# Decode attention on one core: where the K and V loads of the third, and the V load of the last step are split, and how many unused matmuls two early steps run

## The chip, the core and the metric

The kernel runs on one core of one Trainium2 chip. Its time is the device time of one execution in microseconds (us). A core has a matmul engine (TensorE, PE in the profile), three engines for other arithmetic (VectorE or DVE, ScalarE or ACT, GpSimd or POOL), a fifth that only issues transfers here (SyncE or SP), and 16 DMA engines that carry what is issued. SBUF is the core's working memory, PSUM the small memory that TensorE writes to.

## The reference

One decoding step of two layers side by side, for a batch of two and a single new token each:

```python
xn = layernorm(x)                                   # x: 2 x 1 x 512
q  = (xn @ wq) as [2, 32, 1, 128]
p  = softmax(q . k_cache * 128**-0.5)               # k_cache: 2 x 32 x 8192 x 128, bf16
o  = p @ v_cache                                    # v_cache: the same shape
out = x + o.reshape(2, 1, 4096) @ wo + relu(xn @ w1) @ w2
```

The two caches hold 134 MB each. The weights have 4.2 MB (wq), 4.2 MB (wo), and 1.8 MB each for w1 and w2.

## The kernel before, in words

The 64 pairs of batch and head are taken four at a time (U = 4), in NP = 16 steps. The code counts them t = 0 to 15, so the "third step" is t = 2. In a step, each of the 128 partitions holds 256 key rows (KB = 256) of one pair: a K tile `ks` and a V tile `vs`, 8.39 MB each. There is one buffer for each, called its slot. There is no second one, so a K tile can be loaded only once the step before has finished with its own.

What TensorE does in a step (lines 306 to 351, one hardware loop, rolled up):

- It waits for the K tile: `dK[0]` before the first half of the transposes, `dK[1]` before the second half.
- 256 transposes (L275) turn the K rows so that the head dimension lies on partitions. They come in 32 groups of 8; VectorE and ScalarE copy each group from PSUM to SBUF (L429). The last transpose of each group counts up a semaphore; group 7, 15, 23 and 31 of a step count up `pT[7]`, so it grows by four in each step.
- 256 score matmuls (L282), with a maximum over each half of the scores (VectorE, L476), then exponentials on ScalarE (L550).
- 256 output matmuls (L335) with V rows as weights. They wait for `dV[0]` before the first half, `dV[1]` before the second. The last matmul of each half counts up `sW`.
- Unless it is the last or last but one step, 24 matmuls of 128x512 into a PSUM tile that nobody reads (L346): the "unused matmuls". `reg` counts the steps from 1, so in step t it holds t + 1.

SyncE issues all loads, one after the other, in an unrolled list (L184 to L194), all into one DMA queue: K of step t, then V of step t. Each issue first waits until the slot is free. `load` (L176) makes either one transfer of the whole tile, once `pT[7]` (for K) or `sW` (for V) says that the whole slot is used up, or two transfers of half a tile, each once its half is used up. `KSPLIT` and `VSPLIT` name the steps whose tiles come in halves. Where a tile comes whole, GpSimd passes its arrival on to the second semaphore (L239), so that TensorE's loop body can be the same in all steps.

Before the loop, wq is loaded into the V slot and q is computed, so V of step 0 waits for that. After the last step's transposes, w1, w2 and wo are loaded into the K slot (wo in four pieces, the later ones smaller), and the end of the program computes both output products and the sum.

## Time and profile before

| | |
|---|---|
| median of 4 runs | 659.97 us (658.18 to 660.2) |
| the profiled execution's own time | 659.18 us |
| its span, first to last instruction | 657.4 us |
| DMA queue 1, share of 16 engines' span | 99.0% |
| read from HBM | 280.50 MB, 427 GB/s over the span |
| TensorE busy, share of the span | 602.5 us, 92% |
| transposes L275, busy | 234.6 us, 4096 |
| output matmuls L335, busy | 141.9 us, 4096 |
| score matmuls L282, busy | 132.5 us, 4096 |
| unused matmuls L346, busy | 74.8 us, 336 |
| mean granted TensorE clock | 0.964 |

A busy time of TensorE is a sum of modelled, pipelined spans; it doesn't mean that the array works at its peak. The DMA rows give the share of time in which the 16 DMA engines have a packet under way. An idle engine matters only if it is on the chain that ends last, so the profile's chain of waits, its stretches of time and its list of what SyncE issued are what the steps below are read from. Times inside the run are counted from the start of the span. The profiled execution's time lies 1.8 us above its span.

### The profile page before, as it was taken

To read this page: it belongs to the slowest core of one execution; us is meant where nothing else is said; L and a number is where in the kernel's file an instruction comes from. 1 tells how busy PE (TensorE), PEld (TensorE's weight loads), DVE (VectorE), ACT (ScalarE), POOL (GpSimd) and SP (SyncE) were. 2 spreads that over 40 slices of the span, in tenths; PEclk is the share of its full clock that TensorE was granted. 3 is DMA by queue.
4 is the path that set the end of the run, shared out by engine and by line. 5 is a ranking of instruction groups with operands and counts; after the bars stand their busy time and mean duration, and the time that the engine had idled before them with its cause. 6 is when DMAs were issued, how large, how long until landed. Compare 5 with 4: busy or idle time off the path is not lost.

```text
span 657.4 us, 27600 instructions
## 1 busy us (share of the span) xinstructions
PE 602.5 (92%) x12987; PEld 547.4 (83%) x12987; DVE 261.9 (40%) x503; ACT 290.9 (44%) x532; POOL 7.2 (1%) x30
## 2 busy tenths in 40 slices
PE   2797999999999999999999999999999999999997
PEld 0596887978889898888979878897987889798987
DVE  1441450716235071632507154260715417072721
ACT  1332443636345263543527354343725435372730
POOL 2000000000000000000000000000000000000000
PEclk9977999999899899999989999998999999999997
DMA  9999999999999999999999999999999999999996
GB/s 381 446 441 425 408 423 447 419 443 439 415 443 431 439 443 419 431 439 439 439 411 435 447 439 435 411 439 447 439 431 411 443 447 439 427 411 435 423 428 281
DMA packets 6223, 280.66 MB, mean 427 GB/s; under 512 B 706, under 2 KB 708, under 8 KB 964
## 3 DMA queue, kind: packets, MB, share of 16 engines
q1 hardware_dynamic: 6208, 280.50, 99.0%
q8 instruction: 8, 0.13, 0.1%
q14 instruction: 3, 0.02, 0.0%
q10 hardware_dynamic: 4, 0.00, 0.0%
HBM read 280.50 MB, written 0.00 MB: 427 GB/s over the span
## 4 chain that ended last, share of the span: by engine, by line
PE 65%; DMA 31%; DVE 2%; issue 1%; SPq 0%; ACT 0%; ACTq 0%
PE tp L275 34%; DMA ks<-in_A_k_cache_dram 27%; PE ot L335 13%; PE Sc L282 11%; PE ms L346 6%; DMA ks<-in_A_wo_dram 4%; DVE mcol L476 2%; PE ms L294 0%; PE ms L300 0%; ACT L429 0%; ACT kT L429 0%; PE Sc L400 0%; SPq L194 0%; SPq L191 0%; SPq L182 0%
## 5 line engine op out<-in xcount | busy, mean ns | idle before, releaser
L429 DVE COPY kT<-tp 128x1024 bf16<-128x1024 bf16 x320 | 209.3, 688 | 252.1 <-PE tp L275 246.5
L275 PEld LDWEIGHTS tp<-identb,ks 128*128 128x128 bf16 x4096 | 232.2, 99 | 16.8 <-DMA ks<-in_A_k_cache_dram 14.9
L275 PE MATMUL tp<-identb,ks 128*128 128x128 bf16 x4096 | 234.6, 220 | 11.4 <-DMA ks<-in_A_k_cache_dram 10.4
L429 ACT COPY kT<-tp 128x1024 bf16<-128x1024 bf16 x192 | 188.2, 1014 | 122.6 <-PE tp L275 122.6
L335 PE MATMUL ot<-prm,vs 128*128 128x64 bf16 x4096 | 141.9, 198 | 2.1 <-issue 2.1
L335 PEld LDWEIGHTS ot<-prm,vs 128*128 128x128 bf16 x4096 | 137.7, 101 | 4.1 <-issue 2.3
L282 PE MATMUL Sc<-q,kT 128*128 128x64 bf16 (+8 forms) x4096 | 132.5, 191 | 1.6 <-issue 1.6
L282 PEld LDWEIGHTS Sc<-q,kT 128*128 128x128 bf16 x4096 | 128.0, 97 | 3.0 <-issue 1.7
L346 PE MATMUL ms<-identb 128*128 128x512 bf16 x336 | 74.8, 379 | 0.0
L476 DVE TENSOR_REDUCE mcol<-Sc 32x1 bf16<-32x128 f32 x128 | 37.1, 289 | 90.2 <-PE Sc L282 88.9
L550 ACT ACTIVATE prm<-Sc,nm 32x128 bf16<-32x128 f32 x128 | 69.0, 539 | 5.4
L545 ACT COPY nm<-ms 128x4 f32<-128x4 f32 x32 | 5.2, 163 | 137.9 <-PE ms L300 137.9
L346 PEld LDWEIGHTS ms<-identb 128*128 128x128 bf16 x336 | 31.9, 98 | 36.4
L561 ACT COPY OTf<-ot 128x8 f32 x16 | 2.7, 166 | 80.2 <-PE ot L335 80.2
L550 ACT ACTIVATION_READ_ACCUMULATOR prm<-Sc,nm x128 | 32.1, 250 | 0.0
L294 PE MATMUL ms<-identb,mcol 128*1 128x128 bf16 x32 | 6.9, 217 | 22.1 <-DVE mcol L476 22.1
L294 PEld LDWEIGHTS ms<-identb,mcol 128*1 128x1 bf16 x32 | 2.5, 79 | 23.9 <-issue 23.1
L429 ACT ACT_TABLE_LOAD x16 | 20.5, 1283 | 3.6 <-issue 3.5
L254 PE MATMUL ot<-vs,xz 128*16 128x512 bf16 x32 | 8.5, 431 | 8.6 <-DMA vs<-in_A_wq_dram 8.6
L483 DVE TENSOR_REDUCE mx<-ms 1x4 bf16<-1x128 bf16 x32 | 8.9, 279 | 13.8 <-PE ms L294 13.8
L254 PEld LDWEIGHTS ot<-vs,xz 128*16 128x16 bf16 x32 | 3.1, 99 | 13.6 <-issue 10.7
L236 POOL COPY q<-qb 128x4 bf16<-128x4 bf16 x16 | 3.0, 188 | 591.4 <-PE Sc L282 573.2
(61 smaller groups left out, 47.5 us busy)
## 6 DMA issues: line engine op xcount, KB each, us to landing
ks<-in_A_k_cache_dram SPq DMA_DIRECT2D x4, 4096.0 KB, 22.9
vs<-in_A_v_cache_dram SPq DMA_DIRECT2D x4, 4096.0 KB, 21.8
vs<-in_A_wq_dram SPq DMA_DIRECT2D x1, 4096.0 KB, 12.2
ks<-in_B_w_dram SPq DMA_DIRECT2D x2, 1792.0 KB, 16.5
ks<-in_A_wo_dram SPq DMA_DIRECT2D x1, 2304.0 KB
ks<-in_A_wo_dram SPq DMA_DIRECT2D x1, 1024.0 KB, 25.9
ks<-in_A_wo_dram SPq DMA_DIRECT2D x1, 512.0 KB, 26.6
ks<-in_A_wo_dram SPq DMA_DIRECT2D x1, 256.0 KB, 26.8
```

The lines of the kernel that those rows point to most:

```text
L236: g.tensor_copy(q4[:], qb[:, U * t:U * t + U]).then_inc(sQ1, 1)
L254: i = pe.matmul(qp, lhsT=xz[:, kt, Z - g * Bsz:Z - g * Bsz + QG * Bsz], rhs=vs[:, (kt * QG + g) * 512:(kt * QG + g + 1) * 512], start=(g = ...
L275: t = pe.transpose(tp[e % 4][:, i, :], ks[:, kk * Dh:(kk + 1) * Dh], identb[:])
L282: t = pe.matmul(Sc[:, U * kk:U * (kk + n)], lhsT=kT[e][:, i, :], rhs=rep(q4[:], n), start=True, stop=True,)
L294: pe.transpose(trp[:, i * P:(i + 1) * P], mcol[:, i:i + 1], identb[:]).then_inc(sT, 1)
L335: t = pe.matmul(oh[:, i, :], lhsT=vs[:, kk * Dh:(kk + 1) * Dh], rhs=rep(prm[:, kk, :], REP), start=(first == 0), stop=(first == KB // 2 - 1),)
L346: pe.matmul(ms[:], lhsT=identb[:], rhs=identb[:].rearrange("p (o k) -> p o k", o=1).to_broadcast([P, 4, P]), start=True, stop=True,)
L429: fn(kT[e][:], tp[e % 4][:]).then_inc(kR[e % HG], 1)
L476: m = v.tensor_reduce(out=mcol[own, i:i + 1], in_=S[own, i * KB // 2:(i + 1) * KB // 2, u], axis=AX.X, op=ALU.max,)
L483: v.tensor_reduce(out=mx[:, i, :], in_=trp[:, i * P:(i + 1) * P].rearrange("o (u m) -> o u m", u=U), axis=AX.X, op=ALU.max, negate=True,). ...
L545: a.copy(nm[:, i, :], bc[:, i, :]).then_inc(sN, 1)
L550: x = a.activation(out=prm[own, k, u], in_=S[own, k, u], func=ACTF.Exp, bias=nm[own, i, u:u + 1], scale=1.0, accum_out=RS[own, i, bass.ds( ...
```

## The change

K2 and V2 (step t = 2) come in two halves, each asked for when that half of its slot is used up. V15 comes whole. TensorE runs 18 unused matmuls in step 0, none in step 1, and 24 in steps 2 to 13 as before. The loop body gets two more branches; the matmuls move into a helper.

```diff
-    KSPLIT = (0, NP - 1)
-    VSPLIT = (1, NP - 1)
+    KSPLIT = (0, 2, NP - 1)
+    VSPLIT = (1, 2)
...
+        def warm(n):
+            for i in range(n):
+                pe.matmul(
+                    ms[:], lhsT=identb[:],
+                    rhs=identb[:].rearrange("p (o k) -> p o k", o=1).to_broadcast([P, 4, P]),
+                    start=True, stop=True,
+                )
...
             with pe.If_lt(reg, NP - 1):
-                for i in range(WARM):
-                    pe.matmul(
-                        ms[:], lhsT=identb[:],
-                        rhs=identb[:].rearrange("p (o k) -> p o k", o=1).to_broadcast([P, 4, P]),
-                        start=True, stop=True,
-                    )
+                with pe.If_ne(reg, 2):
+                    warm(WARM - WARM // 4)
+                    with pe.If_ne(reg, 1):
+                        warm(WARM // 4)
             advance(pe, regs)
```

## The prediction

> Steps are numbered t = 0 to 15 as in the code's loops; K1 is the K tile of step 1, K2a the first half of K2. Added or lost time is in us.

> **What bounds the kernel.** First I read the DMA rows of the page.

> ```profile
> DMA  9999999999999999999999999999999999999996
> ...
> q1 hardware_dynamic: 6208, 280.50, 99.0%
> ...
> HBM read 280.50 MB, written 0.00 MB: 427 GB/s over the span
> ```

> One queue carries everything and its packets fill 99.0% of the span, so only time in which that queue runs dry can be won or lost. Next, stretches of the span (columns: busy us of each engine with its count, granted clock, DMA share, GB/s).

> ```profile
> 90.00:95.00 5.00, 5.00 (x157) 4.81 (x154) 1.44 (x5) 0.16 (x1) 0.00 (x0) 1.00 0.98 406
> 95.00:127.00 32.00, 29.42 (x597) 26.11 (x594) 13.89 (x25) 17.89 (x32) 0.19 (x1) 1.00 1.01 436
> ...
> 170.00:605.00 435.00, 414.28 (x8994) 377.03 (x8991) 177.72 (x338) 203.38 (x382) 2.26 (x12) 0.97 1.00 433
> ```

> From 170 to 605 us the queue runs at 433 GB/s without a hole; a K or V tile is 8.39 MB, so it takes 19.36 and a step of two tiles 38.7. Around 90 to 95 us, 406 GB/s shows a hole. The chain of waits and SyncE's issues say why:

> ```profile
> 73.74 14.31 PE tp L275 x256
> 88.06 24.17 DMA ks<-in_A_k_cache_dram
> ...
> 126.78 24.16 DMA ks<-in_A_k_cache_dram
> 150.94 0.05 issue
> 150.98 14.47 PE tp L275 x256
> ```
> ```profile
> 88.06 0.33 SPq L182 DMA_DIRECT2D ks<-in_A_k_cache_dram  x1
> 105.94 0.33 SPq L182 DMA_DIRECT2D vs<-in_A_v_cache_dram  x1
> 126.78 0.33 SPq L182 DMA_DIRECT2D ks<-in_A_k_cache_dram  x1
> 144.65 0.33 SPq L182 DMA_DIRECT2D vs<-in_A_v_cache_dram  x1
> 165.48 0.33 SPq L182 DMA_DIRECT2D ks<-in_A_k_cache_dram  x1
> ```

> The K slot is single: K2 is asked for when step 1's transposes end (88.06), K3 at 126.78, K4 at 165.48. The trace's packet records, followed on the slowest of the 16 DMA engines, give these ends: V1 91.72, K2 111.90, V2 131.22, K3 150.53, V3 169.85. Every tile takes 19.32 to 19.36 except K2, which takes 20.18. So the K request needs a **lead** over the end of the tile ahead of it: 91.72-88.06 = 3.66 was too little and cost 0.82; 131.22-126.78 = 4.44 and 169.85-165.48 = 4.37 cost nothing, nor did the smallest later lead that I worked out, 4.17 at K6. The kernel lives on about 0.3 of spare lead. TensorE, with its 24 unused matmuls, fits the same 38.7 nearly exactly.

> **The change, part by part.** *Step 0, 18 unused matmuls for 24.* Step 0's row is 5.18 for 24, so 0.216 each; 6 fewer are 1.30. K1's last landing is at 72.76 and step 1 now begins at 73.74, so 0.94 is won on TensorE, the rest is waiting. K2's request moves from 88.06 to 87.1.

> *K2 in halves.* K2a is asked for 7.2 into step 1's transposes, at 80.0, K2b at 87.1; both stand in the queue before V1 ends. The hole at 90 us closes. Price: half tiles have 32 KB packets, 1.213 each, against 2.42 for 64 KB, and a tile of halves takes 19.42 (K15, V15) against 19.36: +0.06. K2 ends at 91.72+19.42 = 111.14 instead of 111.90: **-0.76**. SyncE's extra issue (0.33) and its wait stand ahead of V2's, which comes some 14 later; nothing else is queued there. GpSimd skips a forwarding wait, nobody waits for it.

> *V2 in halves*: +0.06 on the queue. Its requests come with the halves of step 1's output matmuls (about 101 and 105), well before K2b is through. *V15 whole*: -0.06. It is asked for at the end of step 14's outputs (second half of the 605.23 issue row, 609.1), 5.8 before K15's last packet at 614.91, so no hole. It lands near 634.8, while step 15's first output matmul now starts at 634.39 on half a tile: TensorE 0.45 later. Its chain meets the last Wo pieces, where it idles 0.28 and 0.22 for DMA: at most 0.1 comes through; I take **+0.05**.

> *Step 1 without unused matmuls.* Outputs end at 105.0 (105.94-0.94). K2a has landed by 102, so step 2 starts at once. What that looks like is shown by step 15, which also follows a step without them:

> ```profile
> 609.24 1.96 PE L275 MATMUL tp<-identb,ks 128*128 128x128 bf16 x32 [0.17 <-issue]
> 609.58 1.28 ACT L429 ACT_TABLE_LOAD   x1 [0.24 <-issue]
> ...
> 611.94 12.51 PEld L275 LDWEIGHTS tp<-identb,ks 128*128 128x128 bf16 x224 [0.92 <-ACT kT L429]
> ```

> The skipping branch costs 0.17, and ScalarE's table load, otherwise under the unused matmuls, now delays the copies: 15.4 for the transposes instead of 14.4. Step 2's transposes end at 120.4, K3 is asked for 6.4 earlier than now, hidden behind V2, which ends at 111.14+19.42 = 130.56. Step 2's outputs end 17.9 after its transposes (144.65-126.78), at 138.3, the 24 unused matmuls at 143.5. Both halves of V2 are there in time.

> K3 cannot come sooner: 130.56+19.35 = 149.9, landed 150.4. **TensorE now idles from 143.5 to 150.4, 6.9**, where it idled 1.18. The six microseconds won in step 2 come back as a wait before a K tile that is whole. The trace shows one such idle, 3.37 before step 0's second K half:

> ```profile
> 34.10 10.16 PE L275 MATMUL tp<-identb,ks 128*128 128x128 bf16 x128 [3.37 <-DMA ks<-in_A_k_cache_dram]
> ```
> ```profile
> 33.30:36.70 3.40, 2.60 (x25) 2.61 (x26) 0.68 (x1) 1.01 (x1) 0.00 (x0) 0.50 1.07 463
> 36.70:40.00 3.30, 3.30 (x34) 3.30 (x32) 1.40 (x3) 1.58 (x2) 0.00 (x0) 0.50 1.10 477
> 40.10:44.00 3.90, 3.90 (x73) 3.90 (x71) 3.42 (x6) 2.85 (x4) 0.00 (x0) 1.00 0.99 424
> ```

> The clock fell to half and stayed there until 40.09 while transposes ran: 10.16 for 128, against 7.16 (half of 14.31): 3.0 lost in 6.0 of half clock. The 1.18 idles show no such fall. After 6.9 I expect the fall surely. Its remainder p is not shown for this place: upper end 3.0, this row; lower end 1.4, from the query matmuls, which start at 13.34 and have full clock from 16.20 in the clock records, 2.9 later, at half loss. I take 2.1, near the middle, since the clock changes only in a grid of 3.41 and nothing fixes the phase.

> So K4 is asked for at 150.36+14.5+p, and V3 ends at 149.91+19.36 = 169.27: lead 4.41-p = 2.3, less than K2's 3.66. **A new hole in the queue before K4.** Its price has two ends. By K2's row, lead 3.66 cost 0.82, each missing us costs one more: 4.48-2.3 = 2.2. But three of the engines got their K2 packets late there (first packets at 91.29 to 92.13, against 89.80 to 90.28 for the other early ones); without those three, the first packet ends 5.2 after the request instead of 6.9, and the price falls by 1.7, to 0.5. I take 1.9, nearer to the row. With both ends of p: 0 to 3.0. TensorE is then late by about as much as the queue, and goes on as now.

> *Sum*: -0.76 + 0.06 - 0.06 + 0.05 + 1.9 = **+1.2**. Against the profiled execution's 659.18 that is 660.4; the median of the runs shown is 659.97, 0.79 above that execution, so the same sum gives **661.2**.

> [...] In these rows the clock rose at 40.09 in the middle of transposes. [...]

> **Rivals.** *A, the hole does not open (faster):* the half clock ends soon after restart (p 1.4) and the engines take K4's packets like the thirteen others at K2: price 0, sum -0.7, **659.3**. For it: the low end of both bounds. Against: both must be low together. Chance 0.20.
> *B, TensorE becomes the bound (slower):* p leaves it late in step 3, and it can only catch up by what it has spare. Over three steps (150.98 to 267.09) it idles 1.02 in 116.11. The steps of 39.0 hold a spell of half clock in the outputs (176.6 to 180.0, records), others none. If a shifted phase puts one into every step, three steps take 117.0, 0.9 more than the DMA's 116.1, four times over: +3.6, on top of 1.2, **664.8**. It decides from a mean step of 38.71 on. Chance 0.08.
> *C, the first hole is not the whole of what K2 lost, or it does not close:* K2a's queueing disturbs V1; then only the new hole shows, +1.9, **661.9**. Against: later halves (K15) came without a loss. Chance 0.06.
> Forecast: 0.66.

> **Numbers.** About 0.3%, 2.0, is what a measurement of this kernel can tell from no change. The forecast runs from -0.7 to +2.3 (659.3 to 662.3); the runs shown scatter by 1 around the median; with A and C inside, the range is 659.0 to 662.9. Faster by over 0.3% (below 658.0) needs more than the queue lost at K2: 0.04. Slower (above 661.95): a quarter of the forecast, B whole, half of C: 0.27. Within: 0.69.

> **What would show it.** Right: no hole at 90 us, K2 landed at 111.6; step 2's transposes from 105.0, about 15.4; TensorE idle of 6 to 7 before step 3 and half clock into it; step 3's transposes 15.8 to 17.5; under 430 GB/s around 166 to 172; later steps 38.7. Wrong: full clock at 150 us, or a K4 that lands 38.7 after K3. A K3 idle under 3 would break the chain at its root.

## The result and the profile after

| | before | after |
|---|---|---|
| median | 659.61 us (78 runs) | 660.80 us (50 runs) |
| ratio, with its 95% interval | | 1.0017 (1.0010 to 1.0024) |
| profiled execution | 659.18 us, span 657.4 | 660.83 us, span 659.0 |

The change costs 1.1 us (0.0017 of 659.6). The forecast was 661.2 us: 1.2 more than the 659.97 of the runs shown first, and 660.8 if the same 1.2 is added to the 659.61 here. In the profiled execution the span is 1.6 longer.

First the DMA queue, in the page of after and in stretches of its span (columns as before: engines, granted clock, DMA share, GB/s).

```profile
q1 hardware_dynamic: 6352, 280.50, 98.7%
```
```profile
90.00:95.00 5.00, 5.00 (x163) 4.88 (x160) 1.44 (x5) 0.00 (x0) 0.00 (x0) 1.00 1.00 433
...
165.00:170.00 5.00, 5.00 (x128) 5.00 (x126) 3.33 (x6) 2.60 (x3) 0.00 (x0) 1.00 0.90 341
...
175.00:605.00 430.00, 401.79 (x8897) 363.29 (x8894) 176.87 (x335) 202.31 (x379) 2.24 (x12) 1.00 1.00 432
```

The hole at 90 us is gone (406 GB/s before, 433 now). A larger one has opened at 165 to 170 us: 341 GB/s. From 175 us on the mean is as before (432 against 433); a second, smaller hole lies in that stretch, before V4, as the landings below show.

Why there? TensorE's timeline of after, then SyncE's issues:

```profile
106.82 1.96 PE L275 MATMUL tp<-identb,ks 128*128 128x128 bf16 x32 [0.36 <-issue]
109.33 12.68 PE L275 MATMUL tp<-identb,ks 128*128 128x128 bf16 x224 [0.55 <-ACT kT L435]
...
139.73 5.34 PE L306 MATMUL ms<-identb 128*128 128x512 bf16 x24
150.53 17.23 PE L275 MATMUL tp<-identb,ks 128*128 128x128 bf16 x256 [5.45 <-DMA ks<-in_A_k_cache_dram]
```
```profile
122.04 0.33 SPq L182 DMA_DIRECT2D ks<-in_A_k_cache_dram  x1
139.92 0.33 SPq L182 DMA_DIRECT2D vs<-in_A_v_cache_dram  x1
167.78 0.33 SPq L182 DMA_DIRECT2D ks<-in_A_k_cache_dram  x1
185.66 0.33 SPq L182 DMA_DIRECT2D vs<-in_A_v_cache_dram  x1
```

Step 2 now begins at 106.82 instead of 112.28, and K3 is asked for at 122.04 instead of 126.78. But K3 lands at 150.48 (before: 150.94), since the queue is full until then (432 GB/s, share 1.00, in the row from 145.10 below). TensorE waits 5.45, and step 3's transposes take 17.23 instead of 14.47. So K4 is asked for at 167.78 instead of 165.48. The clock in the same stretch of after:

```profile
145.10:149.50 4.40, 0.00 (x0) 0.00 (x0) 0.00 (x0) 0.00 (x0) 0.00 (x0) 1.00 1.00 432
149.60:156.30 6.70, 5.78 (x55) 5.78 (x56) 2.08 (x3) 2.46 (x3) 0.00 (x0) 0.50 1.06 460
156.40:600.00 443.60, 416.77 (x9216) 378.30 (x9215) 187.97 (x352) 208.94 (x378) 2.05 (x11) 1.00 1.00 431
```

For most of TensorE's idle time the clock still stands at full; it falls between 149.5 and 149.6, about 1 us before the idle time ends, and stays at half for 6.8.

**Where the 1.6 of the span came from.** I follow the last landing of each tile in the trace, after minus before. K1: +0.10 (72.86 against 72.76). K3: -0.46, so -0.56 between the two, the closed hole less the price of the halves. V3: -0.46. K4: +0.31, so +0.77 here. V4: +0.72, another +0.41, since V4 too is asked for late (185.66 against 184.83). From there to V15 (+0.68) nothing changes. The last Wo piece is at +1.19: 0.51 come up in the last 7.9 MB. That stretch from V15 to the last Wo piece took 18.4 to 19.7 in the profiles of this study (24.95 in that of experiment 1), without an order that I could see. The rest, 0.36, lies behind TensorE's last work, in the result's own transfer: from its issue to the end of the span it took 2.83 against 2.46, and 2.82 in the profile of experiment 5, which changes nothing there. I count these two sums as scatter. The change itself: -0.56 + 0.77 + 0.41 = +0.6 in this execution.

### The profile page after: what moved, and what is told of

Its sections match the earlier page's. It is cut to its first block, busy times and chain, and to the rows that moved or that the text cites. A ratio compares the mean times of both kernels' runs of the same rounds, so it can differ in the third digit from the quotient of the medians.

```text
span 659.0 us, 27567 instructions
## 1 busy us (share of the span) xinstructions
PE 590.8 (90%) x12957; PEld 537.1 (82%) x12957; DVE 262.0 (40%) x503; ACT 290.8 (44%) x532; POOL 7.1 (1%) x30
## 2 busy tenths in 40 slices
DMA  9999999999999999999999999999999999999996
## 3 DMA queue, kind: packets, MB, share of 16 engines
q1 hardware_dynamic: 6352, 280.50, 98.7%
HBM read 280.50 MB, written 0.00 MB: 426 GB/s over the span
## 4 chain that ended last, share of the span: by engine, by line
DMA 50%; PE 46%; issue 1%; DVE 1%; ACT 1%; SPq 0%; ACTq 0%
DMA ks<-in_A_k_cache_dram 46%; PE tp L275 34%; PE ot L343 5%; PE Sc L282 5%; DMA ks<-in_A_wo_dram 4%; PE ms L306 1%; DVE mcol L482 1%; ACT L435 0%; ACT kT L435 0%; PE ms L294 0%; PE Sc L406 0%; SPq L194 0%; PE ms L300 0%; SPq L191 0%; SPq L182 0%
## 5 line engine op out<-in xcount | busy, mean ns | idle before, releaser
L275 PEld LDWEIGHTS tp<-identb,ks 128*128 128x128 bf16 x4096 | 233.1, 99 | 29.1 <-DMA ks<-in_A_k_cache_dram 26.2
L275 PE MATMUL tp<-identb,ks 128*128 128x128 bf16 x4096 | 236.2, 221 | 22.4 <-DMA ks<-in_A_k_cache_dram 20.6
L282 PE MATMUL Sc<-q,kT 128*128 128x64 bf16 (+8 forms) x4096 | 134.0, 192 | 3.4 <-issue 3.4
L343 PE MATMUL ot<-prm,vs 128*128 128x64 bf16 x4096 | 131.5, 193 | 2.2 <-issue 1.8
L282 PEld LDWEIGHTS Sc<-q,kT 128*128 128x128 bf16 x4096 | 129.6, 98 | 4.7 <-issue 3.5
L343 PEld LDWEIGHTS ot<-prm,vs 128*128 128x128 bf16 x4096 | 127.5, 98 | 4.2 <-issue 1.9
L306 PE MATMUL ms<-identb 128*128 128x512 bf16 x306 | 68.9, 382 | 0.0
L306 PEld LDWEIGHTS ms<-identb 128*128 128x128 bf16 x306 | 29.2, 98 | 33.6 <-issue 1.0
```

Of the source, the lines that this page charges most:

```text
L275: t = pe.transpose(tp[e % 4][:, i, :], ks[:, kk * Dh:(kk + 1) * Dh], identb[:])
L282: t = pe.matmul(Sc[:, U * kk:U * (kk + n)], lhsT=kT[e][:, i, :], rhs=rep(q4[:], n), start=True, stop=True,)
L306: pe.matmul(ms[:], lhsT=identb[:], rhs=identb[:].rearrange("p (o k) -> p o k", o=1).to_broadcast([P, 4, P]), start=True, stop=True,)
L343: t = pe.matmul(oh[:, i, :], lhsT=vs[:, kk * Dh:(kk + 1) * Dh], rhs=rep(prm[:, kk, :], REP), start=(first == 0), stop=(first == KB // 2 - 1),)
```

## The experiments

The theory: the unused matmuls that step 1 no longer runs come back as idle time before K3; TensorE's clock falls; step 3's transposes and all behind them come late; so requests for K4 and V4 come late, and the queue runs dry. The rival: the halves of K2 and V2, or the early K3 request, leave the 16 DMA engines in an order that opens the hole. Ratios are against runs of the kernel before that were measured alongside. "Run 6" below means the run of experiment 6.

**1. Fill the idle time of step 2.**

```diff
                     with pe.If_ne(reg, 1):
                         warm(WARM // 4)
+                    with pe.If_eq(reg, 3):
+                        warm(22)
```

> The changed kernel with 22 more unused matmuls in step 2 (22 x 0.216 = 4.75 us of the 5.45 us for which TensorE idled before K3). Theory (an idle TensorE falls to half clock, step 3's transposes take 17.2 instead of 14.4, so K4 is asked for too late and the queue runs dry): no half clock at 150 us, transposes of step 3 14.5, no hole at 165 to 170 us, K4's last packet about 0.9 and V4's about 0.3 us earlier; about 1.2 us faster than the changed kernel, so 0.2 to 0.8 faster than before, ratio 0.9988 to 0.9997. Rival (the hole comes from the halves of K2 and V2, or from K3 having been asked for early, which leaves the 16 DMA engines in another order): the hole at 165 to 170 us stays and the time is that of the changed kernel, ratio 1.0017.

Measured: 913.86 us, ratio 1.388 (1.382 to 1.394). Neither theory speaks of this. The page's DMA queues, and TensorE's timeline:

```profile
q8 instruction: 143, 2.34, 1.1%
```
```profile
131.09 5.33 PE L275 MATMUL tp<-identb,ks 128*128 128x128 bf16 x49 [10.62 <-issue]
```

Before, the row was `q8 instruction: 8, 0.13, 0.1%`. A step of the loop holds 1592 matmuls and weight loads (256 of each of three kinds, 4 small ones and 24 unused, twice). 22 more with their weights, 44 instructions that run in one step only, make it 1636, and now the loop's code is loaded again and again: 2.34 MB instead of 0.13. TensorE stands still meanwhile, 10.62 ahead of step 2 alone, although K2 had landed at 114.55. The run says nothing on the hole. The 135 more loads are nine for each of the loop's 15 repeats if they fall evenly (an estimate from the two rows), 16 KB each (2.34 MB over 143). So the run shows that this body no longer stayed loaded; at which size that begins it doesn't show.

**2. The same fill with less code.** Loops of six matmuls replace the written-out ones:

```diff
-                    warm(WARM - WARM // 4)
+                    with pe.Fori(0, 3):
+                        warm(6)
                     with pe.If_ne(reg, 1):
-                        warm(WARM // 4)
+                        warm(6)
+                    with pe.If_eq(reg, 3):
+                        with pe.Fori(0, 3):
+                            warm(6)
```

> The changed kernel with 18 more unused matmuls in step 2 (3.9 us of the 5.45 us of idle time), this time from small loops of 6, so that the code of TensorE's loop body is shorter than before, not longer (22 written out took the instruction loads from 0.13 to 2.34 MB and the time to 914 us). Theory: TensorE idles 1.5 to 3 us before K3 and keeps full clock, step 3's transposes take 14.5, no hole at 165 to 170 us: 0.9 to 1.3 us faster than the changed kernel, ratio to before 0.9997 to 1.0003, as V15 still comes whole. Rival (halves or the early K3 request make the hole): the hole stays, ratio 1.0017. If the small loops cost, idle time named issue stands before L306.

Measured: 659.96 us, ratio 1.0006 (0.9988 to 1.0024); instruction loads 0.13 MB again. The fill was too short in this profile: idle 2.79 before K3, and the clock still fell, for 3.4. K4 landed in time, V4 1.27 late. So the expectation of full clock failed, and 2.79 is not short enough. The next run has 24 more (`Fori(0, 4)`) instead of 18.

> The changed kernel with 24 more unused matmuls in step 2 from small loops of 6 (18 more left 2.79 us of idle time in the profile and the clock still fell for 3.4 us, with no hole at K4 and one of 1.3 at V4). Theory: idle before K3 0.3 to 2 us, full clock through step 3, K4's and V4's landings each 19.35 after the tile ahead, time 0.5 to 1.5 us under the changed kernel's in the same call. Rival (order of the DMA engines after the halves): K4 or V4 still late by 0.8 to 1.3, time as the changed kernel.

Measured: median 659.81 us, ratio 0.9991 (0.9972 to 1.0011); the changed kernel, measured alongside (below), 660.57, and the kernel before 659.67. TensorE's timeline of this kernel:

```profile
139.07 10.52 PE L306 MATMUL ms<-identb 128*128 128x512 bf16 x48
150.38 14.47 PE L275 MATMUL tp<-identb,ks 128*128 128x128 bf16 x256 [0.79 <-DMA ks<-in_A_k_cache_dram]
```

With 0.79 of idle time the transposes take 14.47 again. K4 is asked for at 164.88 and lands 19.35 after V3, V4 19.34 after K4. Halves, whole V15, and the early K3 request are all still there: the rival is out. By the medians the 24 matmuls bring 0.76 back of the 0.90 that the changed kernel loses here; the two intervals overlap from 1.0005 to 1.0011.

**3. The changed kernel once more,** alongside the run with 24. No edit.

> The changed kernel as it is, so that it shares its runs of the kernel before with the next three. Theory: TensorE idles 5 to 7 us before K3, half clock into step 3, transposes 15.8 to 17.3, K4's landing more than 19.35 us after V3's or V4's more than 19.35 after K4's, by 0.8 to 1.3 in sum; ratio 1.0010 to 1.0024. Rival (the 1.0017 was scatter between chips): ratio 0.9997 to 1.0005.

Measured: 660.57 us, ratio 1.0016 (1.0005 to 1.0027). The idle time before K3 is 6.67 here; of the 6.8 of half clock (147.2 to 154.1) 3.3 lie inside the idle time, and the transposes take 16.13. K4 lands in time, V4 0.67 late. So the loss moves between K4 and V4 from execution to execution.

**4. Put step 1's unused matmuls back.**

```diff
-                with pe.If_ne(reg, 2):
-                    warm(WARM - WARM // 4)
-                    with pe.If_ne(reg, 1):
-                        warm(WARM // 4)
+                warm(WARM - WARM // 4)
+                with pe.If_ne(reg, 1):
+                    warm(WARM // 4)
```

> The changed kernel with the 24 unused matmuls of step 1 put back; the halves of K2 and V2, the whole V15 and the 18 of step 0 stay. Theory: step 2 starts 5.2 us later, TensorE idles about 1 us instead of 5.45 before K3, the clock stays full, no hole at K4; no hole at 90 us either, since K2 is asked for in halves. 0.2 to 0.8 us faster than before (ratio 0.9988 to 0.9997). Rival (the halves and the early K3 request do it): K2 and V2 still come in halves, so the hole at 165 us stays, ratio about 1.0017.

Measured: 660.04 us, ratio 1.0010 (1.0001 to 1.0019). The profile has what the theory wants (idle 1.27 before K3, transposes 14.47, no hole at K4; from K2 to V15 the landings are 0.2 to 0.3 earlier than before), but the time has not: the end is late. TensorE's timeline of this kernel at the end:

```profile
634.60 1.89 PE L343 MATMUL ot<-prm,vs 128*128 128x64 bf16 x32 [0.42 <-DMA vs<-in_A_v_cache_dram]
...
636.54 7.47 PE L343 MATMUL ot<-prm,vs 128*128 128x64 bf16 x224
...
651.18 3.55 PE L405 MATMUL Sc<-OX,ks 128*128 128x2 bf16 x128
```

A whole V15 is waited for, 0.42, and a spell of half clock (634.4 to 637.8) lengthens the two rows of outputs, 1.14 and 6.93 before. TensorE ends its 128 Wo matmuls without a wait, at 654.73, 1.1 after the last Wo piece has landed (653.64); before, it was 0.4 (654.13 after 653.71). (The 1.7 and 1.1 in the expectation of the run with V15 alone count from the last but one piece.) So I tried V15 both ways.

```diff
-    VSPLIT = (1, 2)
+    VSPLIT = (1, 2, NP - 1)
```

> The changed kernel with step 1's 24 unused matmuls put back and the last V in halves again, so K2 and V2 in halves and 18 unused matmuls in step 0 are all that is left of the change. Theory (the hole at K2 is closed for 0.7 us, and what the kernel with a whole V15 lost again it lost at the end): 0.3 to 0.9 us faster than before, ratio 0.9986 to 0.9995. Rival (V15 costs nothing, and halves or 18 matmuls cost what was won): ratio about 1.001, as with the whole V15.

Measured, on top of experiment 4's edit: 659.76 us, ratio 0.9999 (0.9981 to 1.0017). And the whole V15 alone in the kernel before, `VSPLIT = (1,)`:

> The kernel before with the last V in one piece, nothing else. Theory 1 (the prediction's term): the end is set by the last Wo pieces from DMA, the later start of step 15's outputs is covered by TensorE's waits of 0.2 to 0.3 us for them: within 0.1 us of before, ratio 0.9998 to 1.0002. Theory 2 (that cover is gone as soon as a spell of half clock falls into step 15's outputs, as in the profile with the unused matmuls of step 1 put back, where TensorE ended 1.7 us after the last Wo piece had landed instead of 1.1): 0.2 to 0.9 us slower, ratio 1.0003 to 1.0014, and TensorE's output matmuls of step 15 wait about 0.4 us for V15.

Measured: 659.76 us, ratio 0.9998 (0.9981 to 1.0015). Its profile has the same wait (0.30) and the same late end (655.1 against 654.1), again with half clock in the outputs. The intervals of the two runs are too wide to tell 0.3 to 0.6 us from nothing. What a whole V15 costs stays open; that it takes TensorE's cover at the end away is seen in both profiles. The other profiles bear this out: leaving out experiment 1, a spell of half clock lies in step 15's outputs in four of the seven with a whole V15 and in none of the six with halves. In those four TensorE starts its last transpose 1.35 to 1.74 after the last Wo piece has landed, in the other three 0.67 to 0.68, before 0.68. The first profile of the changed kernel and the one of experiment 3 are among the three. So a part of the 1.1 may be V15's, in executions that were not profiled.

The profile with V15 in halves again shows something else. Step 1's matmuls are back, but TensorE idles 2.76 before K3 all the same:

```profile
150.48 16.09 PE L275 MATMUL tp<-identb,ks 128*128 128x128 bf16 x256 [2.76 <-DMA ks<-in_A_k_cache_dram]
```

The clock is at half for 3.4 of it and K4 is asked for at 166.60, 3.19 before V3 lands. Yet K4 lands 19.35 after V3 and V4 is 0.04 late. A slow step need not cost anything.

**5. K2 alone in halves.** `KSPLIT = (0, 2, NP - 1)` in the kernel before.

> The kernel before with K2 alone in halves. Theory: the hole at 90 to 95 us closes, K2's last packet lands 0.7 to 0.8 us earlier against K1's, and everything behind it too: 0.5 to 0.8 us faster than before, ratio 0.9988 to 0.9993. Rival (the slowest engine would have caught up later, or the end hides it): ratio 0.9997 to 1.0003.

Measured: 659.97 us, ratio 1.0005 (0.9987 to 1.0023). In the profile K3 lands at 150.57, 0.37 earlier than before, with no hole at 90 us. In the time nothing of it can be told.

**6. The missing unused matmuls alone**, the kernel before with a condition around its loop:

```diff
             with pe.If_lt(reg, NP - 1):
-                for i in range(WARM):
+                with pe.If_ne(reg, 2):
+                    for i in range(WARM):
```

> The kernel before without the 24 unused matmuls of step 1; K2 and V2 whole, V15 in halves. Theory (the missing unused matmuls do the harm, wherever the wait falls): TensorE now idles 6.3 us before K2, half clock into step 2, transposes of step 2 15.8 to 17.3 instead of 14.5, so K3 or V3 lands 0.4 to 1.3 late, and K2's hole of 0.8 stays: 0.4 to 1.3 us slower than before, ratio 1.0006 to 1.0020. Rival (halves needed for the harm): ratio 0.9997 to 1.0003.

Measured: 660.86 us, ratio 1.0025 (1.0009 to 1.0040). No halves are needed for the harm. TensorE's timeline and SyncE's issue of this kernel:

```profile
111.60 15.80 PE L275 MATMUL tp<-identb,ks 128*128 128x128 bf16 x256 [6.42 <-DMA ks<-in_A_k_cache_dram]
```
```profile
87.33 0.33 SPq L182 DMA_DIRECT2D ks<-in_A_k_cache_dram  x1
```

The profiled execution was the quickest of its kernel (658.93 us): 6.8 of half clock, 2.8 of it among the transposes, and no late landing; K3, asked for 3.48 before V2 landed, cost nothing. So where the other executions lose their time is not seen; that it is the same chain is argued from experiments 2 and 7. The profile also has no hole at 90 us, although K2 is whole: step 1 began at 72.84 instead of 73.74, K2 was asked for at 87.33 instead of 88.06. So the hole that the change was to close is not there in every execution of the kernel without it. In the two other profiles with a whole K2 it cost 0.70 (V15 alone, K2 asked for at 88.08) and 1.93 (run 7, asked for at 89.88). Step 0's spells of half clock lie elsewhere here (49.6 to 53.0 and 63.2 to 66.7, against 33.3 to 40.1 and 57.2 to 64.0 before); that they move step 1's start is argued, not shown.

**7. No unused matmuls from step 2 on**, `If_lt(reg, 3)` in the kernel before: the same harm in twelve steps.

> The kernel before, with the unused matmuls in steps 0 and 1 only; K and V as before. Theory: in each step from 3 on TensorE idles some 5 us before K, falls to half clock, its transposes take 15.8 to 17.3 and each K request comes 1.4 to 2.9 later against the end of the V ahead of it (a lead of 1.6 to 3.0 instead of 4.4); a hole of 0 to 0.9 us in each of 12 steps, at step 3 one of 0.9 as in the changed kernel: 4 to 12 us slower than before, ratio 1.006 to 1.018. Rival (half clock doesn't matter, the changed kernel's hole came from the halves): no hole, within 1 us of before.

Measured: 672.72 us, ratio 1.0196 (1.0175 to 1.0217): 13 us, a little above the 4 to 12 expected. Its timeline:

```profile
152.78 15.91 PE L275 MATMUL tp<-identb,ks 128*128 128x128 bf16 x256 [6.49 <-DMA ks<-in_A_k_cache_dram]
193.15 16.19 PE L275 MATMUL tp<-identb,ks 128*128 128x128 bf16 x256 [5.10 <-DMA ks<-in_A_k_cache_dram]
232.14 17.13 PE L275 MATMUL tp<-identb,ks 128*128 128x128 bf16 x256 [3.44 <-DMA ks<-in_A_k_cache_dram]
```

Each step from 3 to 14 idles 3.4 to 7.1 and has slow transposes. Steps begin 40.4 and 39.0 apart instead of 38.7.

**8. The same, with K in halves in all steps:** `KSPLIT = tuple(range(NP))` on top of 7.

> As the kernel with the unused matmuls in steps 0 and 1 only, and with K in halves in all steps. TensorE still idles before K and falls to half clock, but each K's first half is asked for 7 us earlier. Theory (only the late K request passes the half clock on to the time): transposes at half clock as in the other kernel, no holes, 13 tiles more in halves at 0.06 = 0.8, less the hole of 0.8 at K2: within 1 us of before, ratio 0.9985 to 1.0015. Rival (half clock makes TensorE itself the bound, whenever K is asked for): as slow as the other kernel, ratio 1.006 to 1.018.

Measured: 659.65 us, ratio 1.0001 (0.9988 to 1.0015). The mean granted clock is 0.934, hardly more than the 0.923 of run 7, and the loss of 13 us is gone. Half clock by itself costs nothing in this kernel; it costs through requests that it delays. One point of the expectation was wrong: with halves TensorE doesn't idle 5 us at once, but about 1.5 before a second half and little before a first, and half clock falls elsewhere too.

**9. K4 in halves too,** `KSPLIT = (0, 2, 4, NP - 1)` in the changed kernel: half clock in step 3, an early K4.

> The changed kernel with K4 in halves too, so that its first half is asked for half a set of transposes earlier. Half clock and slow transposes in step 3 stay as they are. Theory (the late K4 request alone passes the half clock on): no hole at 165 to 170 us, K4's second half lands 19.4 after V3; V4, asked for after step 3's late outputs, may still lose 0.3 to 1.3; time 0.3 to 1.0 us under the changed kernel's in the same call. Rival (half clock slows TensorE, and TensorE is the bound): time as the changed kernel.

Measured: 660.81 us, ratio 1.0016 (1.0005 to 1.0027); no better than the changed kernel (660.57). K4's second half lands 19.41 after V3, so that hole is closed, but V4 lands 1.56 late. SyncE's issues in this kernel:

```profile
159.37 7.47 SPq L182 DMA_DIRECT2D ks<-in_A_k_cache_dram  x2
185.87 0.33 SPq L182 DMA_DIRECT2D vs<-in_A_v_cache_dram  x1
```

V4 is asked for at 185.87, after step 3's outputs, late by as much as TensorE is. So "the late K4 request alone" falls: the half clock makes both requests late, K4's and V4's, and one of the two pays. In this profile a second spell of half clock (177.7 to 181.1) adds to it, in step 3's outputs. The two lines are these outputs, here and in the first profile of the changed kernel, which has no such spell:

```profile
177.43 8.41 PE L343 MATMUL ot<-prm,vs 128*128 128x64 bf16 x224
```
```profile
178.69 6.93 PE L343 MATMUL ot<-prm,vs 128*128 128x64 bf16 x224
```

The profiles of the fill of 18 and of run 3 have it too, 8.41 each, and in these three V4 pays 0.67 to 1.56. The kernel before has one at the same place (176.6 to 180.0) and asks for V4 at 184.83, 4.82 before K4 lands, without a loss: there the transposes were quick. So the larger losses at V4 went with two spells in one step, one in the transposes and one in the outputs; the 0.41 of the changed kernel's first profile came with one, behind a K4 that was late itself. In run 8 TensorE starts each step on a half tile, so its outputs come earlier too: V4 is asked for at 179.65 there, against 184.83 in the kernel before.

## Why the prediction was right, and which terms were not

- *The hole at 90 us closes.* Right in the profile, 0.56 between K1 and K3, against 0.70 (0.76 less 0.06 for V2). Wrong as a term for every execution: run 6 has no such hole in the kernel without the halves, and run 5 (0.9987 to 1.0023) can't tell a gain of this size from none. I took one execution's hole for the kernel's. That the half-clock spells, whose phase I allowed for only in p, also move step 1's start would explain it, but is not shown.
- *Step 0's 18 matmuls, step 1 from 72.8.* In the profile after it began at 74.29, with other spells of half clock in step 0; in the second profile of the same kernel at 72.93.
- *Step 2 without cover: 15.4 for its transposes, ending at 120.4.* 106.82 to 122.04 is 15.2, with the wait for ScalarE's copies (0.55 in the timeline above) that step 15 had shown.
- *Idle 6.9 before K3.* 5.45 and 6.67 in two profiles; the first is short by step 1's late start, and under the 6 to 7 that was to show the forecast right.
- *p between 1.4 and 3.0, taken as 2.1.* 2.8 (17.23 less 14.47) and 1.7 (16.13). The grid of 3.41 is in the clock records of both traces, before and after: every stretch but the last, which runs to the end, lasts a whole multiple of it (at half clock 3.41 and 6.83, in after 10.24 too). Its phase against the idle time did differ: in the changed kernel's two profiles the clock fell 4.5 and 3.3 after the idle time before K3 began.
- *The price of the hole, 1.9 at K4; TensorE "goes on as now" behind it.* This term was mis-sized and incomplete. It was 0.77 at K4 and 0.41 at V4 in the first profile, 0 and 0.67 in the second. With the queue empty, K4's first packets began 0.96 to 1.92 after the request, and ended 4.93 after it at the latest, not 6.9 as K2's did. At K4 the lower end of the bound was the better one. And V4's request was late as well, which the prediction left out; run 9 shows that V4 pays when K4 doesn't.
- *The lead as a measure.* Counted from the request to the landing of the tile ahead, leads of 4.64 and more cost nothing in the kernel before. Below that, no single curve fits: 3.14 (run 3) and 3.19 (fill of 18) cost nothing at K4, 3.13, 3.17 and 3.31 cost 0.67, 1.27 and 1.56 at V4. It isn't K against V either: in run 7 K4 cost 1.66 at 3.36 and K12 3.35 at 2.23, but K10 only 0.02 at 2.55. So "each missing us costs one more" and "about 0.3 of spare lead" were both read from too few rows, and what decides the price at a given lead stays open.
- *V15 whole, +0.05.* On the path of the profile after it costs nothing: TensorE waits 0.42 for V15, and later still 0.15 and 0.20 for Wo. In the profiles of experiment 4, with step 1's matmuls put back and with V15 alone, the cover is gone. As a term it depends on whether half clock falls into step 15's outputs.
- *Half clock that ends among transposes.* Borne out: in the profile after it ended at 156.3, while step 3's transposes ran (150.53 to 167.76).
- *The sum.* +1.2 was forecast and 1.1 measured, but that is partly luck: a gain that only some executions have (0.7) against a loss that was put too high (1.9 against 1.2). In the profile the change makes +0.6; the runs say 1.1, and what makes the difference (V15, a dearer hole in other executions) is not shown.

No version beat the kernel before beyond its interval. The best, with 48 unused matmuls in step 2, is at 0.9991 (0.9972 to 1.0011). There is little to win: the queue's packets filled 99.0% of the span before.

## What to carry to other kernels

In this kernel one transfer queue is full (99.0% of the span) and every slot has a single buffer, and time won on the engine ahead of a transfer was not kept: it came back as a wait at the next whole tile (5.45 before K3), the clock fell in that wait (to half, for 6.8), the requests behind it came late, and the full queue got a hole (0.77 at K4, 0.41 at V4) that was not made up later (V4 +0.72, V15 +0.68). So in a kernel of this shape look past the hole that an edit closes to the next wait, and ask which requests the waiting engine issues. And before a hole of 0.8 us in a single profile is priced, look whether it is in a second execution too.
